# A query phi ahead of the products with 1/den: reordering VectorE and ScalarE in a linear-attention kernel

## The chip, the cores and the metric

One core of a Trainium2 chip (trn2). The metric is the device time of one execution in microseconds; lower is better. Every run quoted here is fast, with a granted TensorE clock of 0.999 or 1.0 (0.996 in one run of before).

Names used throughout: `0q23.phi` is layer 0, query projection, group 2, block 3, the step that ends the feature map phi; `.exp`, `.id1` and `.ts` are the steps ahead of it. `0d02`, `0d23` and the like are the short matmuls (128x8 on a timeline) of such a block (group 0 block 2, group 2 block 3) with `Zm`, the masked sum of the key features; together they make the denominators. `0d0` is the denominator of query group 0, and its three steps are `den` (add and take the reciprocal), `rep` (ScalarE replicates 1/den) and `rT` (a DMA transposes the replica). `0d0.pqn` to `0d0.pqn3` are VectorE's four products of the queries with 1/den. `0G0` to `0G3` are the evacuations of the accumulated matrix G out of PSUM, `0v` the matmuls that use it, `0m` and `0M` the next matmuls and their evacuations, `0r2` the replication of 1/den by matmul, `0w3` the first output tile, and `1u011` the first matmul of the feed-forward layer that follows (`1u011.tanh`, `1x6.sq` and `1x6.vpe` are steps of that layer and of its layer norm). The same code has line numbers that differ by a few between the kernels (L409 and L407, for example).

## The reference

```python
def _A_ref(x, wqkv, wo):          # linear attention, 32 heads of 16
    phi = lambda t: jnp.where(t > 0, t + 1, jnp.exp(t)) + 1e-6
    pq, pk = phi(q), phi(k)
    kv  = jnp.einsum("bhsd,bhse->bhde", pk, v)
    z   = jnp.einsum("bhsd->bhd", pk)
    num = jnp.einsum("bhqd,bhde->bhqe", pq, kv)
    den = jnp.einsum("bhqd,bhd->bhq", pq, z)[..., None] + 1e-6
    return (num / den) @ wo       # heads joined again
# x: 2048 x 512, bf16
x = x + A(layernorm(x));  x = x + B(layernorm(x))   # B: silu(x Wg) * (x Wu) @ Wd, 1792 wide
x = x + A(layernorm(x));  x = x + B(layernorm(x))   # layers 0, 1, 2, 3
```

## The kernel before

The kernel is a list of operations with their reads and writes. TensorE runs them in the order of one list (`PROGRAM`), the other engines each in an order of their own (`ORDER`); waits on semaphores follow from the reads and writes. An engine stops at an operation whose inputs are missing, with all that is behind it: in the profile of before TensorE stood 1.33 us at 0d23; VectorE stood 1.83 us at 0d0.pqn2, and 0q23.phi, whose inputs were ready at about 49.3, started behind it at 51.40; ScalarE stood 1.70 us at 0d1.rep1, to 51.11, and the evacuations of G started behind it at 51.64. The parts that matter here, shortened and simplified:

```python
# phi: exp and, if chosen, "+1" on ScalarE; min and max on VectorE
op("act", exp,  r=[pb], w=[e]);  if on_act: op("act", id1, r=[pb], w=dk)
op("dve", ts,   r=[e],  w=[e])
if on_act: op("dve", phi, r=[e] + dk, w=dk)        # two SBUF inputs
else:      op("dve", phi, r=[pb, e],  w=dk)        # reads PSUM

# den: after the reciprocal, for each of 4 token tiles
q = r_rrep.take()                                   # 3 buffers for 4 tiles: the 4th waits
op("act", rep, r=[rtok], w=[rrep[q]])
op("sp",  rT,  r=[rrep[q]], w=[RT_tl], dma=True)    # DMA transpose
op("dve", pqn, r=ks + [RT_tl], w=ks)                # queries times 1/den
```

```
PROGRAM (TensorE): ... 0q23 0d20 0g15 0g12 0g14 0d23 0d22 0d21 0q30 0v 0q31 0m0..0m3 0r2 0w3 0w2 ...
act:  ... 0d0.rep3 0q23.exp 0q23.id1 0d1.rep1 0G0.evac 0G2.evac 0G3.evac 0d1.rep 0q30.id1 ...
dve:  ... 0q23.ts 0d0.pqn2 0q23.phi 0G1.evac 0d0.pqn1 0d2.den 0d2.den1 0d0.pqn3 0v.mask ...
sp:   ... 0d0.rT 0d0.rT2 0d0.rT1 0d0.rT3 ...
```

Of the kernel before, what the change touches and what calls it, by code (L numbers as in the profile page):

```python
# [8 lines left out]
P = 128  # L9
# [155 lines left out]

PROGRAM = """
# [22 lines left out]
0x14.stats 0x14.sq 0k6.exp 0k7.exp 0k6.id1 0q03.exp 0x11.apply 0k8.id1 0k8.exp 0k15.exp 0k15.id1 0k13.exp 0k12.exp  # L189
0k13.id1 i.c 0k11.exp 0q11.id1 i.c1 0q11.exp 0k14.id1 0k14.exp 0q02.exp 0q02.id1 0q10.exp 0q01.id1 0q01.exp 0q00.exp  # L190
i.c3 0q12.id1 0q12.exp i.c2 0q21.exp 0q21.id1 0q13.id1 0q13.exp 0d0.rep 0d0.rep2 0q20.exp 0d0.rep1 0q22.exp 0d0.rep3
0q23.exp 0q23.id1 0d1.rep1 0G0.evac 0G2.evac 0G3.evac 0d1.rep 0q30.id1 0q30.exp 0q31.exp 0q31.id1 0M1.evac 0M3.evac
0d1.rep3 0d1.rep2 1x3.sq 1x2.sq 0q33.id1 1x1.sq 0q33.exp 1x0.sq 0q32.exp 1x5.sq 0q32.id1 1x11.sq 1x7.sq 1u011.tanh
1u007.tanh 1x6.sq 1u005.tanh 1u008.tanh 1u002.tanh 1u006.tanh 1x6.apply 1x9.sq 1u012.tanh 1u003.tanh 1u013.tanh
# [22 lines left out]
i.c 0x0.stats 0x0.aggr 0x0.vpe 0x1.stats 0x1.aggr 0x0.apply 0x3.stats 0t0.xT 0x4.stats 0x3.aggr 0x4.aggr 0x1.apply  # L217
# [3 lines left out]
0x12.apply 0x14.vpe 0k7.ts 0k6.ts 0k7.phi 0q03.ts 0k9.ts 0k9.phi 0k6.phi 0q03.phi 0x14.apply 0k8.ts 0k12.ts 0k15.ts  # L221
0k8.phi 0k15.phi 0k12.phi 0k13.ts 0k11.ts 0k13.phi 0k11.phi 0k14.ts 0q11.ts 0q02.ts 0k14.phi 0q11.phi 0q02.phi
0q10.ts 0q10.phi 0q01.ts 0q01.phi 0q00.ts 0q00.phi 0z.zm 0q12.ts 0d0.den 0d0.den1 0q13.ts 0q12.phi 0q13.phi 0q21.ts
0q21.phi 0q20.ts 0q20.phi 0d1.den 0q22.ts 0d1.den1 0q22.phi 0q23.ts 0d0.pqn2 0q23.phi 0G1.evac 0d0.pqn1 0d2.den
0d2.den1 0d0.pqn3 0v.mask 0q30.ts 0d2.den2 0d1.pqn1 0M0.evac 0M2.evac 0d0.pqn 0r2.pqn 0w3.res 0r2.pqn1 0w2.res
0r2.pqn2 1x3.apply 0r2.pqn3 0w1.res 1x2.apply 0w0.res 0d1.pqn3 0d1.pqn2 0q33.ts 1x1.apply 0q33.phi 0d1.pqn 0w5.res
1x0.apply 0w11.res 0w9.res 1x5.vpe 0w7.res 0w6.res 0q32.ts 1x5.apply 0w4.res 1x11.vpe 0w10.res 1x7.vpe 1u011.gst
0w8.res 1u011.h 0q31.ts 1x11.apply 0q31.phi 0q30.phi 1u007.gst 1u007.h 1x6.vpe 1u005.gst 1u008.gst 1u008.h 1u005.h
0q32.phi 1u006.gst 1u006.h 1u002.gst 1u002.h 1u012.gst 1x7.apply 1u012.h 1u003.gst 1x4.vpe 0d3.den 1x4.apply 1u003.h
1x9.apply 1u013.gst 0d3.den1 1u013.h 1u010.gst 1u010.h 1u004.gst 1u004.h 1u000.gst 1u000.h 1u001.gst 1u001.h  # L230
1u009.gst 1u009.h 1u110.gst 0d3.pqn 0d3.pqn2 0w14.res 1u110.h 1n3.res 0d3.pqn3 1n1.res 1u102.gst 1n0.res 0w12.res
1u102.h 1n2.res 1u106.gst 1u106.h 0d3.pqn1 2x2.vpe 2x2.apply 1u107.gst 0w13.res 1u204.gst 2x1.vpe 1u107.h 1u101.gst
0w15.res 2x0.vpe 1u204.h 1u101.h 1u111.gst 2x0.apply 1u111.h 1u105.gst 1u109.gst 2k2.ts 1u109.h 2x3.apply 1x14.apply
1u103.gst 1u103.h 1u105.h 1u108.gst 1u108.h 1u104.gst 1u104.h 1u100.gst 1u100.h 1u113.gst 1u112.gst 2k0.ts 1x12.vpe
1u113.h 1u112.h 1n6.res 2k2.phi 1n7.res 2q00.ts 1x15.vpe 1x13.vpe 2k3.ts 2k0.phi 2k0.zs 1u209.gst 2x6.vpe 1x15.apply
1u209.h 1n4.res 1u211.gst 1x12.apply 1u211.h 2x4.vpe 1u205.gst 1n5.res 2x4.apply 1u213.gst 1u205.h 2k1.ts 1u200.gst
1u200.h 1u303.gst 1u213.h 1u202.gst 1u303.h 1u202.h 1u203.gst 1u203.h 1u208.gst 2k1.phi 1u301.gst 1u309.gst 1u208.h
1u301.h 1u304.gst 1u206.gst 1u309.h 1u304.h 1u206.h 1u212.gst 1u212.h 1u201.gst 1u201.h 2k3.phi 1u311.gst 1u311.h
1u302.gst 2q00.phi 2q10.ts 1u302.h 2q11.ts 2q11.phi 1u305.gst 1u305.h 1u207.gst 1u207.h 2q10.phi 1u310.gst 1u310.h
1u308.gst 1u308.h 1u312.gst 1u312.h 1u210.gst 1u210.h 2q02.ts 1n11.res 1u313.gst 1u313.h 2q02.phi 2q01.ts 1u300.gst  # L240
2q03.ts 1n8.res 1u300.h 1n10.res 2x8.vpe 2q03.phi 2k4.ts 2k4.phi 2x10.vpe 1u306.gst 1n9.res 1u306.h 2x11.apply
1u307.gst 2q01.phi 1u307.h 1n14.res 2k8.ts 2k10.ts 2k8.phi 2k8.zs 2k7.ts 2k7.phi 2k10.phi 2k10.zs 1n15.res 2k5.ts
2k6.ts 2k5.phi 2k9.ts 2q21.ts 2x15.vpe 2q21.phi 2k6.phi 2k11.ts 2k11.phi 2x15.apply 2k9.phi 1n13.res 2x13.vpe
1n12.res 2k9.zs 2x13.apply 2q12.ts 2q12.phi 2k15.ts 2k15.phi 2x12.apply 2k14.ts 2k14.phi 2q20.ts 2q20.phi 2k13.ts
2q22.ts 2k13.phi 2q22.phi 2k12.ts 2k12.phi 2k12.zs 2s.zh 2s.zl 2z.zm 2q13.ts 2q23.ts 2q23.phi 2q13.phi 2d0.den
2d0.den1 2d1.den 2q31.ts 2d2.den 2d2.den1 2d0.pqn 2q30.ts 2d1.den1 2d0.pqn1 2q30.phi 2d1.den2 2q31.phi 2G1.evac
2r1.pqn 2d0.pqn2 2r1.pqn1 2v.mask 2r1.pqn2 2r1.pqn3 2M3.evac 2q32.ts 2d0.pqn3 2q33.ts 2w0.res 2q32.phi 2q33.phi
2w2.res 3x0.apply 2w1.res 2d2.pqn3 2d2.pqn 3x2.apply 2w3.res 2w6.res 3x1.apply 2w11.res 2d2.pqn1 3x3.apply 2d2.pqn2
2w5.res 2d3.den 2w8.res 2w7.res 2w4.res 3x11.vpe 3x6.vpe 3x11.apply 2w10.res 3u008.gst 2w9.res 3x6.apply 3u000.gst
3u008.h 3x7.vpe 3u009.gst 3u000.h 3u009.h 3u013.gst 3x5.apply 3u013.h 3x4.apply 3x7.apply 3u010.gst 3u004.gst  # L250
3u010.h 3u004.h 3u003.gst 3u005.gst 2d3.den1 3u005.h 3u003.h 3u007.gst 3u103.gst 3u110.gst 3u007.h 2d3.pqn1 3u103.h
3x9.vpe 3u110.h 2d3.pqn 3u108.gst 3u002.gst 3u108.h 3u012.gst 3u012.h 3u002.h 3u006.gst 3u001.gst 3u006.h 3x9.apply
# [13 lines left out]
0x8.pow 0x15.pow 0x12.pow 0x13.vpe 0x13.pow i.c1 0x13.negm 0x11.pow 0x11.nmr 0x12.negm 0x14.pow 0x14.negm i.ld i.ld1  # L266
i.ld2 i.ld3 i.ld4 i.ld5 i.ld6 i.ld7 i.ld8 i.c7 1x3.negm 1x3.vpe 1x3.pow 1x2.negm 1x2.vpe 1x2.pow 1x1.negm 1x1.vpe
1x1.pow 1x0.negm 1x0.vpe 1x0.pow 1x11.negm 1x5.pow 1x7.negm 1x5.negm Wd.ld3 1x9.negm 1x7.pow 1x6.negm 1x11.pow
Wd.ld1 Wd.ld2 1x4.negm 1x6.pow 1x10.negm Wd.ld 1x6.nmr 1x8.negm 1x9.vpe 1x9.pow 1x4.pow 1x10.vpe 1x10.pow 1x10.nmr
1x8.vpe 1x8.pow 1x8.nmr 2x2.negm 2x0.negm 1x14.negm 2x1.negm 2x2.pow 2x1.pow 2x3.vpe 2x3.negm 2x3.pow 2x0.pow  # L270
2x1.nmr 1x14.vpe 1x14.pow 1x12.pow 2x6.negm 2k2.zs 1x13.negm 1x12.negm 2x7.vpe 1x13.pow 1x15.pow 2x7.negm 1x15.negm
2x7.pow 1x13.nmr 2x6.pow 2x4.pow 2x6.nmr 2x4.negm 2x7.nmr 2x5.vpe 2x5.negm 2x5.pow 2x5.nmr 2k1.zs 2x11.negm 2k3.zs
2x8.negm 2x8.pow 2x8.nmr 2x11.vpe 2x10.negm 2k4.zs 2x11.pow 2x10.pow 2x9.negm 2x10.nmr 2x9.vpe 2x9.pow 2x9.nmr
2x14.negm 2x14.vpe 2x14.pow 2x14.nmr 2k7.zs 2k5.zs 2x15.pow 2x15.negm 2k6.zs 2x13.pow 2x13.negm 2x12.vpe 2x12.pow
2x12.negm 2k11.zs 2k15.zs 2k14.zs 2k13.zs 3x0.negm 3x0.vpe 3x0.pow 3x2.negm 3x2.vpe 3x2.pow 3x1.negm 3x1.vpe 3x1.pow
3x3.negm 3x3.vpe 3x3.pow 3x11.negm 3x11.pow 3x4.negm 3x5.vpe 3x6.negm 3x5.negm 3x6.pow 3x5.pow 3x7.pow 3x7.negm
3x4.vpe 3x4.pow 3x8.vpe 3x8.negm 3x8.pow 3x9.negm 3x9.pow 3x13.negm 3x10.vpe 3x14.negm 3x10.pow 3x12.pow 3x12.negm
3x10.negm 3x10.nmr 3x13.pow 3x13.nmr 3x15.pow 3x14.vpe 3x15.negm 3x14.pow
# [3 lines left out]
0x8.xT 0x15.xT 0x13.xT 0x12.xT 0x11.xT 0x14.xT 0d0.rT 0d0.rT2 0d0.rT1 0d0.rT3 0d1.rT1 0d1.rT 0d1.rT3 0d1.rT2 1x3.xT  # L282
# [8 lines left out]


PE_T = set("""
0d2 0t0 0t1 0t2 0t3 2d1 2z
""".split())



ON_ACT = set("""
0G0 0G2 0G3 0M1 0M3 0k10 0k13 0k14 0k15 0k6 0k8 0k9 0p0 0p11 0p12 0p14 0p7 0q01 0q02 0q11 0q12 0q13 0q21 0q23 0q30  # L300
0q31 0q32 0q33 0s10 0s12 0s13 0s14 0s15 0s2 0s7 0t1 0t12 0t13 0t14 0t2 0t3 0t4 0t5 0t6 0t7 0x11 1p11 1p12 1p13 1p15
1p4 1p5 1p6 1p7 1t0 1t10 1t13 1t14 1t3 1t8 1x10 1x13 1x6 1x8 2G0 2G2 2G3 2M0 2M1 2M2 2b0 2b10 2b12 2b8 2b9 2k0 2k1
2k15 2k2 2k3 2k4 2k5 2k7 2k8 2k9 2p0 2p1 2p10 2p13 2p15 2p2 2p4 2p6 2p8 2q00 2q01 2q02 2q03 2q10 2q11 2q13 2q21 2q22
2q23 2q31 2q32 2q33 2t10 2t14 2t15 2t5 2x1 2x10 2x14 2x5 2x6 2x7 2x8 2x9 3p11 3p12 3p13 3p15 3p6 3p7 3p9 3t0 3t10
3t3 3t4 3t6 3t7 3t8 3x10 3x13
""".split())


def bass_interleave_layers__linear_attn_block__swiglu_ffn__prompt_kernel(
    nc: bass.Bass,  # L310
    A_x: bass.AP,
    A_wqkv: bass.AP,
    A_wo: bass.AP,
    B_x: bass.AP,
    B_w_gate: bass.AP,
# [14 lines left out]
    with stack:  # L330
# [8 lines left out]
        ones = sb("ones", [P, 1], BF16)  # L339
# [240 lines left out]
        def k_proj(L, t):  # L580
# [8 lines left out]
            if f"{L}z" in PE_T:  # L589
                assert L == 0 or all(f"{L - 2}w{i}" in given for i in range(T))  # L590
                z_add(L, t)
# [333 lines left out]
```

## Time and profile before

| | before |
|---|---|
| time, median of the first 3 runs | 429.98 us (429.4 to 430.33) |
| span of the profiled execution | 428.1 us |
| TensorE busy | 419.4 us, 98% |
| longest TensorE idle in the stretch concerned | 1.33 us, ahead of 0d23 |
| stretch from the start of 0d02 to the start of 0w3 | 42.56 to 56.60: 14.04 us |

Busy shares tell only that TensorE sets the time and that there is little idle time to win. What matters is where its idle time lies and who ended it. A timeline line gives start, length, engine, source line, operation, output and inputs, shape and count; in square brackets stands the idle time ahead of it and the operation that ended it. The lines are shown in the prediction.

### The profile page before, as it was taken

Reading aid. Unit: us, or ns where it says so; the run is one execution under the profiler, and the core shown is the slowest. Engines: PE = TensorE matmul, PEld = TensorE weight load, DVE = VectorE, ACT = ScalarE, POOL = GpSimd, SP = SyncE. Lnnn points to the kernel's source line nnn. Section 1 sums busy time; section 2 is a strip of 40 time slices with the busy share of each in tenths; the row PEclk is TensorE's granted clock in tenths of the full one; section 3 lists DMA queues with packets and bytes.
Section 4 is the critical chain, followed back from the end, with each engine's and each line's share of the span. In section 5 each row is a group of like instructions: output and inputs, shape, how many; then the busy total and the mean of one; then the engine's idle time right before and its main releaser. Section 6 shows DMA issues by size and latency. Waiting matters only on the chain.

```text
span 428.1 us, 6340 instructions
## 1 busy us (share of the span) xinstructions
PE 419.4 (98%) x2219; PEld 195.5 (46%) x2219; DVE 287.8 (67%) x629; ACT 202.9 (47%) x399; POOL 83.0 (19%) x205
## 2 busy tenths in 40 slices
PE   8999899999999999999999999999999999999997
PEld 6444444444444444444444444344444444444443
DVE  6865799793675476875447869888837606853662
ACT  5998785563356264254465648445312302402220
POOL 5634035210120150001334500431002000100000
PEclk9999999999999999999999999999999999999999
DMA  8639534522011021000021113322110010021001
GB/s 277 141 75 329 126 64 101 146 50 51 4 22 37 2 52 34 2 0 2 2 48 26 25 26 63 62 46 41 38 38 0 13 51 25 0 63 37 2 0 50
DMA packets 53279, 23.21 MB, mean 54 GB/s; under 512 B 46528, under 2 KB 52160, under 8 KB 53248
## 3 DMA queue, kind: packets, MB, share of 16 engines
q1 hardware_dynamic: 51408, 16.27, 17.6%
q0 software_dynamic: 1296, 6.03, 4.1%
q10 hardware_dynamic: 544, 0.52, 0.4%
q8 instruction: 17, 0.28, 0.3%
q14 instruction: 14, 0.11, 0.1%
HBM read 9.70 MB, written 2.10 MB: 28 GB/s over the span
## 4 chain that ended last, share of the span: by engine, by line
PE 88%; DMA 5%; ACT 3%; DVE 2%; issue 1%; SPq 0%; POOL 0%; ACTq 0%; DVEq 0%
PE pb L409 88%; DMA RT<-rrep 2%; DMA xnT<-xnA 1%; DMA X<-in_A_x_dram 1%; ACT pq L567 1%; ACT etmp L564 1%; ACT rrep L719 0%; DVE pq L573 0%; ACT GT L657 0%; DVE pq L732 0%; SPq L723 0%; ACT xnA L498 0%; SPq L440 0%; DVE xnA L522 0%; ACT xnA L495 0%
## 5 line engine op out<-in xcount | busy, mean ns | idle before, releaser
L782 ACT ACTIVATE tht<-pb 128x512 f32<-128x512 f32 x112 | 65.4, 595 | 129.4 <-PE pb L409 106.8
L409 PE MATMUL pb<-xnT,Wg 128*128 128x512 bf16 x448 | 115.0, 379 | 0.6 <-issue 0.6
L409 PE MATMUL pb<-xnT,Wu 128*128 128x512 bf16 x448 | 115.0, 379 | 0.0
L784 DVE SCALAR_TENSOR_TENSOR tht<-tht,pb 128x512 f32<-128x512 f32 x112 | 75.4, 684 | 55.6 <-ACT tht L782 48.9
L409 PE MATMUL pb<-Wd,hT 128*128 128x512 bf16 (+2 forms) x462 | 99.8, 373 | 0.0
L787 DVE TENSOR_TENSOR hT<-tht,pb 128x512 bf16<-128x512 f32 x112 | 74.2, 682 | 2.8
L409 PEld LDWEIGHTS pb<-Wd,hT 128*128 128x128 bf16 x462 | 44.7, 98 | 52.3 <-DVE hT L787 0.2
L409 PEld LDWEIGHTS pb<-xnT,Wu 128*128 128x128 bf16 x448 | 43.6, 98 | 53.1 <-DVE hT L787 0.8
L409 PEld LDWEIGHTS pb<-xnT,Wg 128*128 128x128 bf16 x448 | 43.5, 98 | 53.3 <-issue 1.3
L511 POOL TENSOR_TENSOR rstd<-vpe,negh 128x1 f32<-128x1 f32 x64 | 37.4, 587 | 90.4 <-DVE vpe L507 88.3
L564 ACT ACTIVATE etmp<-pb 128x512 bf16<-128x512 f32 x64 | 37.2, 594 | 21.8 <-PE pb L409 13.1
L501 POOL TENSOR_SCALAR mv<-sums 128x1 f32<-128x1 f32 x55 | 12.8, 239 | 119.8 <-DVE X L810 62.1
L409 PE MATMUL pb<-Wqkv,xnT 128*128 128x512 bf16 x128 | 31.2, 379 | 1.2 <-DMA xnT<-xnA 0.6
L409 PE MATMUL pb<-xnT,Wqkv 128*128 128x512 bf16 x128 | 32.1, 379 | 0.0
L409 PE MATMUL pb<-pk,xnA 128*128 128x512 bf16 x128 | 31.2, 379 | 0.0
L409 PE MATMUL pb<-GT,pq 128*128 128x512 bf16 x128 | 30.2, 379 | 0.2
L498 ACT ACTIVATE xnB<-X,sums 128x512 bf16<-128x512 bf16 x32 | 22.9, 717 | 15.7 <-DVE X L762 8.8
L569 DVE TENSOR_SCALAR etmp<-etmp 128x512 bf16<-128x512 bf16 x64 | 18.7, 304 | 12.1 <-ACT etmp L564 12.0
L762 DVE SCALAR_TENSOR_TENSOR X<-pb,X 128x512 bf16<-128x512 f32 x32 | 21.6, 686 | 7.1 <-PE pb L409 7.0
L810 DVE SCALAR_TENSOR_TENSOR X<-pb,X 128x512 bf16<-128x512 f32 x16 | 11.0, 689 | 19.1 <-PE pb L409 19.0
L498 ACT ACTIVATE xnA<-X,sums 128x512 bf16<-128x512 bf16 x23 | 16.5, 717 | 12.1 <-DVE X L810 11.9
L810 DVE SCALAR_TENSOR_TENSOR pq<-pb,X 128x512 bf16<-128x512 f32 (+2 forms) x17 | 10.9, 656 | 14.4 <-PE pb L409 14.3
(77 smaller groups left out, 309.9 us busy)
## 6 DMA issues: line engine op xcount, KB each, us to landing
out_dram<-pq SPq DMA_DIRECT2D x15, 128.0 KB, 1.8
Wg<-in_B_w_gate_dram POOLq DMA_DIRECT2D x4, 448.0 KB, 4.9
Wu<-in_B_w_up_dram POOLq DMA_DIRECT2D x4, 448.0 KB, 4.6
X<-in_A_x_dram SPq DMA_DIRECT2D x6, 256.0 KB, 4.8
Wd<-in_B_w_down_dram POOLq DMA_DIRECT2D x3, 512.0 KB, 4.7
Wqkv<-in_A_wqkv_dram SPq DMA_DIRECT2D x2, 512.0 KB, 7.0
Wqkv<-in_A_wqkv_dram ACTq DMA_DIRECT2D x2, 256.0 KB, 3.5
X<-in_A_x_dram SPq DMA_DIRECT2D x4, 128.0 KB, 3.4
```

Of the source, the lines that this page charges most:

```text
L409: return op("pe", lambda e: e.matmul(o_ap, lhsT=lhsT, rhs=rhs, start=start, stop=stop, skip_group_check=skip), r=r, w=w, n=n)
L498: op("act", lambda a: a.activation(out=b_ap, in_=X[:, t, :], func=ACT.Square, scale=-float(D), bias=sums[:, t:t + 1], accum_out=mv[:, t, 1 ...
L501: op("pool", lambda p: p.tensor_scalar(out=mv[:, t, 0:1], in0=sums[:, t:t + 1], scalar1=-1.0 / D, scalar2=None, op0=ALU.mult), r=[f"sm{t}" ...
L511: op("pool", lambda p: p.tensor_tensor(out=rstd[:, t:t + 1], in0=vpe[:, t:t + 1], in1=negh[:], op=ALU.pow), r=[f"vp{t}", "negh"], w=[f"rs{ ...
L564: op("act", lambda a: a.activation(out=etmp[e][:], in_=PB[pb][:], func=ACT.Exp), r=[f"pb{pb}"], w=[f"e{e}"], kind="exp")
L567: op("act", lambda a: a.activation(out=dst, in_=PB[pb][:], func=ACT.Identity, bias=onep[:]), r=[f"pb{pb}", "onep"], w=dk, kind="id1")
L569: op("dve", lambda v: v.tensor_scalar(out=etmp[e][:], in0=etmp[e][:], scalar1=1.0, scalar2=1e-6, op0=ALU.min, op1=ALU.add), r=[f"e{e}"], w ...
L762: op("dve", lambda v: v.scalar_tensor_tensor(out=X[:, t, :], in0=PB[pb][:], scalar=1.0, in1=X[:, t, :], op0=ALU.mult, op1=ALU.add, accum_o ...
L782: op("act", lambda e: e.activation(out=tht[a][:], in_=PB[pg][:], func=ACT.Tanh, scale=0.5), r=[f"pb{pg}"], w=[f"th{a}"], kind="tanh")
L784: op("dve", lambda v: v.scalar_tensor_tensor(out=tht[a][:], in0=tht[a][:], scalar=1.0, in1=PB[pg][:], op0=ALU.add, op1=ALU.mult), r=[f"pb{ ...
L787: op("dve", lambda v: v.tensor_tensor(out=hT[h][:, j, :], in0=tht[a][:], in1=PB[pu][:], op=ALU.mult), r=[f"pb{pu}", f"th{a}"], w=[f"h{h}_{ ...
L810: op("dve", lambda v, pb=pb, lo=lo, hi=hi: v.scalar_tensor_tensor(out=o_ap[:, lo:hi], in0=PB[pb][:, 0:hi - lo], scalar=0.5, in1=X[:, t, lo ...
```

## The change

It is meant to let the last query phi that TensorE needs (0q23.phi) run before VectorE takes up the products with the first 1/den, and to evacuate G before ScalarE turns to the second 1/den. Neighbouring operations on all engines are rearranged with it, up to about 75 us. TensorE's list stays word for word, and the `z_mm` part of the diff only rewrites how the sums for z are emitted. The core of the diff (cut; `...` stands for what is left out):

```diff
 act
-0d0.rep3 0q23.exp 0q23.id1 0d1.rep1 0G0.evac 0G2.evac 0G3.evac 0d1.rep 0q30.id1 ...
+0q23.exp 0d0.rep3 0G0.evac 0G1.evac 0G3.evac 0d1.rep 0d1.rep1 0q30.id1 ...
-1u011.tanh 1u007.tanh 1x6.sq 1u005.tanh
+1u007.tanh 1u011.tanh 1x6.sq 1u005.tanh
 dve
-0q23.ts 0d0.pqn2 0q23.phi 0G1.evac 0d0.pqn1 0d2.den 0d2.den1 0d0.pqn3 0v.mask
+0q23.ts 0q23.phi 0d0.pqn 0G2.evac 0d2.den 0d0.pqn1 0d2.den1 0v.mask 0d0.pqn3
 sp
-0d0.rT 0d0.rT2 0d0.rT1 0d0.rT3 0d1.rT1 0d1.rT
+0d0.rT 0d0.rT1 0d0.rT2 0d0.rT3 0d1.rT 0d1.rT1
 ON_ACT
-0G2 0k15 0q23 ...   +0G1 0k11 ...      (0q23.phi now reads PSUM)
 ... (many more moves of the same kind ahead of and behind these)
```

## The prediction

> **What bounds the kernel now.** I read the page first (busy times, slices), then the chain of waits that ended last, then the timeline from 42 to 72 us engine by engine, then the DMA window from 48 to 51.1 us.
>
> ```profile
> PE 419.4 (98%) x2219; PEld 195.5 (46%) x2219; DVE 287.8 (67%) x629; ACT 202.9 (47%) x399; POOL 83.0 (19%) x205
> PE   8999899999999999999999999999999999999997
> PEclk9999999999999999999999999999999999999999
> ```
>
> TensorE is busy 419.4 of 428.1 us at full clock. Only the 8.7 us in which it idles can be won by reordering: 8.7 / 430 = 2.0%, all of it, start and end included. The chain of waits tells where:
>
> ```profile
> 45.23 1.19 SPq L723
> ...
> 46.51 4.53 DMA RT<-rrep
> 51.04 0.02 issue
> 51.06 0.04 DVE pq L732
> ...
> 51.40 0.43 DVE pq L573
> 51.83 0.05 issue
> 51.88 3.15 PE pb L409 x36
> ```
>
> One DMA transpose of the replicated 1/den (line 723) takes 4.53 us, then VectorE multiplies by it (L732), then makes a query phi (L573), and only then TensorE goes on. The timeline of PE and of VectorE there:
>
> ```profile
> 47.79 2.75 PE L409 MATMUL pb<-pk,xnA 128*128 128x512 bf16 x12
> 51.88 0.46 PE L409 MATMUL pb<-Zm,pq 128*128 128x8 bf16 x12 [1.33 <-DVE pq L573]
> ```
> ```profile
> 48.94 0.28 DVE L569 TENSOR_SCALAR etmp<-etmp 128x512 bf16<-128x512 bf16 x1
> 51.06 0.43 DVE L732 TENSOR_TENSOR pq<-pq,RT 128x512 bf16<-128x512 bf16 x1 [1.83 <-DMA RT<-rrep]
> 51.40 0.42 DVE L573 TENSOR_TENSOR pq<-pq,etmp 128x512 bf16<-128x512 bf16 x1
> ```
>
> VectorE's list says 0q23.ts, 0d0.pqn2, 0q23.phi. The product 0d0.pqn2 waits for its transpose, and 0q23.phi, whose inputs were ready at about 49.3 (ScalarE's id1 ran 48.73 to 49.3), stands behind it. TensorE needs that phi for 0d23. ScalarE loses the same stretch to the same transpose: 0d1.rep1 reuses a buffer that it reads, and the evacuations of G stand behind it:
>
> ```profile
> 51.11 0.63 ACT L719 ACTIVATE rrep<-rtok 128x512 bf16<-128x512 bf16 x1 [1.70 <-issue]
> 51.64 1.55 ACT L657 ACTIVATE GT<-pb 128x512 bf16<-128x512 f32 x3
> ```
>
> Why 4.53 us, where transposes elsewhere take 2.4? In the DMA window 48 to 51.1, beside the transposes' small packets, there is one large one:
>
> ```profile
> q8 instruction: 1, 0.02, 1.9%
> ```
>
> In the trace's landings, 15 of the 16 increments of this transpose came by 48.94 and the last at 51.04; the one 16 KB instruction packet ran 49.03 to 49.98. I read it as a collision on one DMA engine. The queue has 17 such packets (0.28 MB), [...] so it should return at the same place of TensorE's program, changed or not.
>
> [...] I count PE gaps between starts (512-column matmuls start 0.216 us apart: 12 in 2.59) and not from busy ends. By this the gap ahead of 0d23 is 51.88 - (47.79 + 2.59) = 1.50, not 1.33.
>
> **The change, part by part.** TensorE's program list is the same word for word. What the heading calls work ahead of the fourth key tile (0g0, 0g1 before 0k3) is already there, and the z_mm part of the diff yields the same matmuls. All that changes is the order on ScalarE, VectorE, GpSimd and SP up to about 75 us, plus a few operations moved from one engine to another.
>
> 1. VectorE: 0q23.phi ahead of all products with the first 1/den; the first of these is now 0d0.pqn, whose transpose landed at 47.63. 0q23 also loses ScalarE's id1, so its phi is the 0.63 us form from PSUM instead of 0.43. Walk from VectorE's Zm at 42.30, with spacings from the timeline (ts 0.21, phi from PSUM 0.6, tensor-tensor 0.34, reciprocal 0.87): den 43.18, reciprocal done 44.63 (0.17 later, because 0q21.ts is inserted), 0q12.phi done 46.15 (TensorE wants it at 46.53: slack 0.38), 0q20.phi 47.0, 0q22.phi 48.2, second reciprocal 49.1, 0q23.phi 49.95. TensorE reaches 0d23 at 47.79 + 2.59 = 50.38. **The 1.50 us gap goes.**
> 2. ScalarE: evacuations of G now precede 0d1.rep and rep1. The last accumulation starts at 49.5 and its four banks fill by 50.58; G0, G1, G3 on ScalarE from 49.95 at 0.5 each end at 51.46, G2 on VectorE at 51.0. TensorE does 0d2x (0.31) and 0q30 (0.86) until 51.55, so 0v starts there (53.05 before).
> 3. 0v 0.94 and 0q31 0.86 end at 53.35. v.mask: 52.69 to 53.3. VectorE in between: 0d2.den, 0d0.pqn1, reciprocal, done by 52.5, provided that pqn1's transpose lands by 51.25. It is issued at about 46.75, and even with the same late increment (51.04) it fits. 0m starts at 53.45 (55.03 before), ends 54.31.
> 4. ScalarE in the meantime: rep, rep1, then 0q30 and 0q31 with two passes each, (51.46 + 6 x 0.53) = 54.6. The fourth matmul of 0r2 reuses the bank that 0q31.exp reads last, so 0r2 loses about 0.3 and ends at 55.25 (56.60 before). M1 and M3 end at 55.6, the last needed at 55.7: 0w3 is held for some 0.2 and ends at 56.11. Before, it started at 56.60 and four matmuls end at 57.46. **Net: 57.46 - 56.11 = 1.35 us.** Before, 50.38 to 56.60 held 6.22 us for 4.45 us of spacing, 1.77 lost; after, 0.4 of it stays.
> 5. Is it kept? TensorE has no visible gap from 56.6 to 98. Tightest places when moved 1.35 forward: 0w11 at 60.43 needs 0r2.pqn3, walked to 60.12; 1u011 at 67.45 needs the last transpose of 1x0, whose apply moved ahead of w5.res and pqn, ending 64.6 (65.98 before, landing 68.46), so landing 67.1. 1u007.tanh now precedes 1u011.tanh on ScalarE, delaying u011.h to 72.6, wanted at 74.36. All hold by 0.3 us or more. After that, the lists are the old ones and everything moves with TensorE.
> 6. The three copies of esel move to about 28 on ScalarE (3 x 0.65); it has caught up by 37.15, where 0q10.exp ran before at 37.14. The tightest bank need, 0q01 for 0k14.id1, holds by 0.5. Off the path. So are x1.apply ahead of x4.aggr and the moved vpe (0.15 each): TensorE's next stop, at 15.69, waits for a transpose that starts with x4.apply at 9.3 either way.
>
> Sum: 429.98 - 1.35 = 428.6.
>
> **The rivals.** (a) The late increment belongs to the profiled execution and not to the timed ones. Then 0d0.pqn2 could start at about 49.2, there was no gap to win, and the time stays at 429.7 or so. For it: a DMA accident, and three runs spread over 0.9 us. Against: [...] the profiled run took 429.86, as the others. One in five. (b) A new wait takes the place of the old: ScalarE's six passes ahead of M1 and M3, or 0d0.pqn1 and pqn3 standing ahead of v.mask and M0.evac when their transposes come late. Slacks are 0.2 to 0.6, so a slip of 1 us would make 429.4. One in five. (c) All slips go well and the 0.4 left over goes too: 428.2. (d) A lost bank or late xnT at 1u011 that makes it slower than before, 430.5: one in twenty.
>
> **Range and chances.** Centre 428.7, a little above the sum because (a) and (b) pull upward; 427.9 to 429.9 also allows for the 0.4 us by which medians of three can move. A 2% change is 8.6 us, all of PE's idle time: 0.01 for faster. Slower by as much would need a stall six times the one removed: 0.01.
>
> **What would show it.** Right: PE's 1.33 us gap ahead of the 128x8 matmuls near 50.4 is gone, 0q23's phi is the form from PSUM and comes before any L732, 0v starts near 51.6, 0w3 near 55.3, 1u011 near 67.5, and the instruction packet is still at 49, now harmless. Wrong: a PE gap between 51.5 and 56 behind ScalarE or L732 of over 0.6 us (rival b), a gap ahead of 1u011 (d), or a kernel before whose other executions lack the late increment (a).

## The result, and the profile after

| | before | changed |
|---|---|---|
| first rounds, median (runs) | 429.69 us (4) | 429.30 us (4) |
| ratio of these rounds | | 0.9991 (0.9974 to 1.0008) |
| repeated later, median (runs) | 429.71 us (10) | 428.68 us (5) |
| ratio of these rounds | | 0.9984 (0.9970 to 0.9998) |
| span of the first profile | 428.1 us | 427.3 us |

The ratios are those for the fast runs of the same rounds; they are not quite the ratios of the medians. The brackets hold a 95% interval. The change is worth between nothing and 1.3 us by the timing, most likely 0.4 to 0.7 us (1 - 0.9991 and 1 - 0.9984 of about 429.7).

Busy time and clock on the page of the changed kernel:

```profile
PE 418.4 (98%) x2219; PEld 194.8 (46%) x2219; DVE 288.3 (67%) x628; ACT 201.8 (47%) x398; POOL 82.6 (19%) x206
...
PEclk9999999999999999999999999999999999999999
```

As before, TensorE is 98% busy at full clock (granted clock 1.0 in both profiles). The timeline of TensorE in the changed kernel, from the last accumulation of G to the first output tile:

```profile
48.53 2.75 PE L407 MATMUL pb<-pk,xnA 128*128 128x512 bf16 x12
51.11 0.45 PE L407 MATMUL pb<-Zm,pq 128*128 128x8 bf16 x12
...
52.28 1.06 PE L407 MATMUL pb<-GT,Wqkv 128*128 128x128 bf16 x16
...
54.12 1.04 PE L407 MATMUL pb<-Wo,KVT 128*128 128x512 bf16 x4
...
55.79 1.90 PE L407 MATMUL pb<-GT,pq 128*128 128x512 bf16 x8
```

The last accumulation starts at 48.53; twelve 512-column matmuls at 0.216 us between starts take 2.59 us, and 0d23 starts right there, at 51.11. The bracket with 1.33 us is gone, and so is any other on these lines. VectorE and ScalarE at the same place:

```profile
50.10 0.69 DVE L574 SCALAR_TENSOR_TENSOR pq<-pb,etmp 128x512 bf16<-128x512 f32 x1
50.71 0.41 DVE L731 TENSOR_TENSOR pq<-pq,RT 128x512 bf16<-128x512 bf16 x1
51.10 0.69 DVE L659 CAST GT<-pb 128x512 bf16<-128x512 f32 x1
```
```profile
50.67 1.58 ACT L656 ACTIVATE GT<-pb 128x512 bf16<-128x512 f32 x3 [0.93 <-PE pb L407]
52.11 1.16 ACT L718 ACTIVATE rrep<-rtok 128x512 bf16<-128x512 bf16 x2
```

0q23.phi is now the form that reads PSUM (`pq<-pb,etmp`, 0.69 us), and it precedes the first product (L731). ScalarE's evacuations of G start as soon as TensorE has the banks ready (0.93 us waited for PE) and no longer behind a replication.

The DMA window from 48.5 to 52 us of the changed kernel still has the large instruction packet in it:

```profile
q8 instruction: 1, 0.02, 1.7%
```

It began at 49.46, after 693 of TensorE's 4438 matmul and weight-load records; in before at 49.03, after 695. Each of the 17 packets began within 38 records of the same packet in the other profile; on average there is one packet per 261 records (4438 / 17).

The stretch from 0d02 to 0w3 fell from 14.04 to 12.50 us (43.29 to 55.79), that is by 1.54. But the whole span fell by only 0.8, because 0d02 started later, at 43.29 in place of 42.56:

```profile
43.29 0.56 PE L407 MATMUL pb<-Zm,pq 128*128 128x8 bf16 x16 [0.36 <-DVE Zm L614]
```

Did the change make the head longer, or do two executions just differ by that much? The experiments had to answer this too.

### The profile page after: what moved, and what is told of

It reads as the page before. It is cut to its first block, busy times and chain, and to the rows that moved or that the text cites. A ratio compares the mean times of both kernels' runs of the same rounds, so it can differ in the third digit from the quotient of the medians.

```text
span 427.3 us, 6331 instructions
## 1 busy us (share of the span) xinstructions
PE 418.4 (98%) x2219; PEld 194.8 (46%) x2219; DVE 288.3 (67%) x628; ACT 201.8 (47%) x398; POOL 82.6 (19%) x206
## 4 chain that ended last, share of the span: by engine, by line
PE 85%; DMA 6%; DVE 3%; ACT 2%; issue 2%; SPq 1%; POOL 1%; POOLq 0%; ACTq 0%; DVEq 0%
PE pb L407 85%; DMA xnT<-xnA 2%; DMA Wu<-in_B_w_up_dram 1%; DMA Wo<-in_A_wo_dram 1%; DMA X<-in_A_x_dram 1%; ACT etmp L562 1%; SPq L722 1%; DMA xnT<-xnB 1%; DMA RT<-rrep 1%; ACT GT L656 0%; ACT rrep L718 0%; DVE stats L486 0%; DVE xnA L520 0%; POOL rstd L509 0%; DVE X L761 0%
## 5 line engine op out<-in xcount | busy, mean ns | idle before, releaser
L499 POOL TENSOR_SCALAR mv<-sums 128x1 f32<-128x1 f32 x55 | 12.5, 234 | 116.7 <-DVE X L809 61.9
```

The costliest lines, as they stand in the source:

```text
L499: op("pool", lambda p: p.tensor_scalar(out=mv[:, t, 0:1], in0=sums[:, t:t + 1], scalar1=-1.0 / D, scalar2=None, op0=ALU.mult), r=[f"sm{t}" ...
```

## The experiments

Twelve runs followed, all correct; c1 and c2 repeat the two kernels unchanged. Each was timed beside the kernel before and profiled once; the last round (e5, e7, e9, e10) ran on another chip than the two rounds ahead of it. In the table, "head" is the start of 0d02, followed by the three stretches in which the rest of the execution can be split; "2nd" and "4th" are the landings of the second and the fourth transpose of 0d0 in the queue: the time of the 15th of their 16 semaphore increments and, after the slash, of the 16th. The first two rows are the two profiles already seen. The last stretch is taken from a span given to 0.1 us, so it is good to 0.05 us.

| kernel | head | 0d02 to 0w3 | 0w3 to 1u011 | 1u011 to end | 2nd | 4th | ratio |
|---|---|---|---|---|---|---|---|
| before | 42.56 | 14.04 | 12.20 | 359.30 | 48.94 / 51.04 | 52.31 / 52.33 | |
| changed | 43.29 | 12.50 | 12.28 | 359.23 | 49.91 / 51.46 | 53.42 / 53.44 | 0.9991 |
| c1 before again | 42.74 | 13.55 | 12.20 | 359.21 | 49.09 / 50.73 | 52.64 / 52.65 | 0.9996 |
| e1 phi only | 42.62 | 13.70 | 12.20 | 359.08 | 49.18 / 50.75 | 52.58 / 52.59 | 0.9986 |
| e2 evac only | 42.90 | 13.82 | 12.19 | 359.09 | 49.25 / 51.19 | 53.15 / 53.16 | 0.9995 |
| e3 phi and evac | 43.32 | 13.09 | 12.41 | 359.58 | 49.66 / 51.49 | 53.45 / 53.46 | 0.9987 |
| e9 three moves | 43.46 | 13.22 | 12.42 | 359.20 | 49.90 / 51.84 | 53.74 / 53.75 | 0.9993 |
| c2 changed again | 42.25 | 12.49 | 12.26 | 359.70 | 50.55 / 50.58 | 52.47 / 52.49 | 0.9984 |
| e4 late product first | 42.41 | 14.20 | 12.25 | 359.24 | 49.03 / 50.81 | 52.75 / 52.76 | 1.0008 |
| e5 landed product first | 43.41 | 12.50 | 12.28 | 359.71 | 50.09 / 51.69 | 53.62 / 53.63 | 0.9984 |
| e6 before, packet moved | 42.98 | 13.42 | 12.53 | 360.67 | 49.33 / 49.35 | 51.98 / 53.97 | 1.0037 |
| e7 changed, packet moved | 42.60 | 12.51 | 12.56 | 362.23 | 49.24 / 49.24 | 51.89 / 53.81 | 1.0043 |
| e8 changed, mask early | 42.31 | 12.49 | 12.25 | 359.95 | 48.95 / 50.55 | 52.48 / 52.50 | 0.9982 |
| e10 later waits | 43.02 | 12.49 | 12.25 | 359.04 | 49.66 / 51.46 | 53.38 / 53.40 | 0.9969 |

The 95% intervals of the ratios reach 0.0012 to 0.0017 to either side.

### c1: the kernel before, once more

> The kernel before once more, unchanged: what two executions differ by. My theory (the wait is in every execution): the 16th increment of the second 1/den transpose again comes about 2 us after the 15th, the gap of 1.3 us ahead of 0d23 is there again, 14.0 us lie between the starts of 0d02 and 0w3 (42.56 to 56.60 before), and 371.5 from there to the end. Rival a (accident of one profile): no gap, about 12.5 to 13. The head, up to 0d02, took 42.56 in the one profile of before and 43.29 in the one of after; if that is noise of the first loads, this run's head may lie anywhere from 42.3 to 43.5; if the change caused it, at 42.5. Ratio 1.000.

No edit. Median 429.41 us, before beside it 429.70 (9 runs): the same kernel read 0.9996, within its interval of 1. TensorE's line at 0d23:

```profile
51.56 0.46 PE L409 MATMUL pb<-Zm,pq 128*128 128x8 bf16 x12 [0.84 <-DVE pq L573]
```

The wait was there again, and the last increment late again (50.73), but the wait was 0.84 us, not 1.33, and the stretch 13.55, not 14.04. So the wait is no accident of one profile; its size moves by half a microsecond from execution to execution. The head was 42.74, and across the six kernels with the old head (before, c1, e1, e2, e3, e9) it ran from 42.56 to 43.46, mean 42.93.

### e1 and e2: either move alone

```diff
 e1, dve
-0q23.ts 0d0.pqn2 0q23.phi
+0q23.ts 0q23.phi 0d0.pqn2
 e2, act
-0q23.id1 0d1.rep1 0G0.evac 0G2.evac 0G3.evac
+0q23.id1 0G0.evac 0G2.evac 0G3.evac 0d1.rep1
```

> Before, with 0q23.phi alone moved ahead of 0d0.pqn2 on VectorE. My theory: TensorE's gap ahead of 0d23 goes (1.5 us by starts), but ScalarE still evacuates G only behind 0d1.rep1, which waits for the same transpose, so 0v can't finish before about 53.9 and 0r2 waits for ScalarE as before: 0d02 to 0w3 shrinks by only 0.1 to 0.3 us (13.8). Rival: VectorE's order was the whole of it, and this alone gives 1.3 to 1.5 us (12.5).

> Before, with the three evacuations of G alone moved ahead of 0d1.rep1 on ScalarE. My theory: the gap ahead of 0d23 stays at 1.3 us and 0d02 to 0w3 stays within 0.2 of 14.0. Rival: ScalarE's order was the whole of it, and this gives 1.3 us or more (12.6).

In e1 the wait ahead of 0d23 went, and TensorE waited for the evacuations of G instead. TensorE's timeline, then ScalarE's:

```profile
52.48 0.23 PE L409 MATMUL pb<-GT,Wqkv 128*128 128x128 bf16 x1 [0.20 <-ACT GT L657]
52.96 0.90 PE L409 MATMUL pb<-GT,Wqkv 128*128 128x128 bf16 x13 [0.26 <-ACT GT L657]
```
```profile
50.82 0.63 ACT L719 ACTIVATE rrep<-rtok 128x512 bf16<-128x512 bf16 x1 [1.18 <-issue]
51.35 1.55 ACT L657 ACTIVATE GT<-pb 128x512 bf16<-128x512 f32 x3
```

The two brackets are the G banks that come late (L657); ScalarE's own line shows why: the replication ahead of them stood 1.18 us (by its times it ends with the second transpose's last increment at 50.75, which frees the replica's buffer). The stretch was 13.70, between the two profiles of before. In e2 the wait ahead of 0d23 stayed:

```profile
52.03 0.46 PE L409 MATMUL pb<-Zm,pq 128*128 128x8 bf16 x12 [1.14 <-DVE pq L573]
```

with a stretch of 13.82. Each half alone is hidden by the other. Timed, e1 read 0.9986 (429.15 us) and e2 0.9995 (429.50 us); e1's ratio is lower than its profile would have it, by an amount the timing can't separate from noise.

### e3: both moves, and e9: a third

> Both moves of the two runs ahead, nothing else of the change. My theory: together they give what neither gives alone: 0d02 to 0w3 falls to 12.4 to 12.8 us, as in the changed kernel (12.50), and the time falls by 1.2 to 1.5 us, ratio 0.9965 to 0.9972, if the head is as in before. Rival: the other moves of the change carry the gain, and this gives less than half of it.

The two edits above together gave 13.09 us: more than either alone, less than the 12.4 to 12.8 expected. TensorE's timeline has a new wait ahead of 0m0:

```profile
55.09 1.02 PE L409 MATMUL pb<-Wo,KVT 128*128 128x512 bf16 x4 [0.61 <-DVE KVT L669]
```

The mask product (L669) stood on VectorE behind 0d0.pqn3, whose transpose landed at 53.46. So e9 added one more move:

```diff
 e9 = e3 and, dve
-0d0.pqn3 0v.mask
+0v.mask 0d0.pqn3
```

> Before with three moves: 0q23.phi ahead of 0d0.pqn2, the evacuations of G ahead of 0d1.rep1, and now also the mask product ahead of 0d0.pqn3, for which TensorE waited 0.61 us in the run of the first two. My theory: these three are the change's whole gain; 0d02 to 0w3 is 12.4 to 12.8 us as in the changed kernel (12.50, 12.49), against 13.09 with two. Rival: the order of the transposes on SP or the other moves matter as well: 12.9 or more.

The stretch did not come down: 13.22 us. My account of three moves was incomplete. VectorE's timeline in e9:

```profile
51.87 0.43 DVE L732 TENSOR_TENSOR pq<-pq,RT 128x512 bf16<-128x512 bf16 x1 [1.05 <-DMA RT<-rrep]
52.21 0.69 DVE L660 CAST GT<-pb 128x512 bf16<-128x512 f32 x1
```

0d0.pqn2, the product of the late transpose, is still the first of the four, and one evacuation of G (L660) stands behind it. It starts at 52.21 and holds 0v on TensorE:

```profile
52.95 1.01 PE L409 MATMUL pb<-GT,Wqkv 128*128 128x128 bf16 x15 [0.28 <-DVE GT L660]
```

The reciprocal and the mask product behind it are late in turn. That e9 is no shorter than e3 lies in the late increment, which came 8.38 us after 0d02 in e9 and 8.17 in e3; from that increment to 0w3 it was 4.84 and 4.92 us. The changed kernel begins with 0d0.pqn instead, the product of the first transpose, and puts the evacuation right after it. By these lines, that order of the products, with the matching order of the transposes on SP, is the part of the gain (13.1 to 12.5) that the moves of the phi and of the evacuations don't bring. No run made that change alone, and the changed kernel differs in other moves too, so this part is argued and not shown. Timed, e3 read 0.9987 (429.04 us) and e9 0.9993 (429.17 us).

### e4 and e5: a product back ahead of the phi

```diff
 e4, changed kernel, dve
-0q23.ts 0q23.phi 0d0.pqn 0G2.evac 0d2.den 0d0.pqn1
+0q23.ts 0d0.pqn1 0q23.phi 0d0.pqn 0G2.evac 0d2.den
 e5, changed kernel, dve
-0q23.ts 0q23.phi 0d0.pqn 0G2.evac
+0q23.ts 0d0.pqn 0q23.phi 0G2.evac
```

> The changed kernel with one product put back ahead of 0q23.phi: 0d0.pqn1, whose transpose is second in the queue and had the late last increment (51.46) in the changed kernel's profile. My theory: VectorE waits for it to about 51.3, 0q23.phi ends near 52.4, and TensorE has a gap of 1.2 to 1.5 us ahead of 0d23: 0d02 to 0w3 is 13.7 to 14.1 us. Rival: any place of the products does, as ScalarE's order is what counts: below 13.0.

> The changed kernel with 0d0.pqn put back ahead of 0q23.phi: a product too, but of the first transpose, whose 16 increments came together in every profile (47.35 to 48.41), long before VectorE gets there (about 50). My theory (what cost time was the one late transpose, not that a product stood ahead of the phi): 0d23 is delayed by 0.1 us at most and 0d02 to 0w3 stays at 12.4 to 12.8, against 14.20 with 0d0.pqn1 there. Rival (any product ahead of the phi costs): 13 or more.

e4's VectorE, then its TensorE:

```profile
50.84 0.42 DVE L731 TENSOR_TENSOR pq<-pq,RT 128x512 bf16<-128x512 bf16 x1 [1.66 <-DMA RT<-rrep]
51.18 0.68 DVE L574 SCALAR_TENSOR_TENSOR pq<-pb,etmp 128x512 bf16<-128x512 f32 x1
```
```profile
51.92 0.46 PE L407 MATMUL pb<-Zm,pq 128*128 128x8 bf16 x12 [1.53 <-DVE pq L574]
```

The product of the late transpose waited 1.66 us, the phi followed it, TensorE stood 1.53 us, and the stretch was 14.20: the whole gain was gone. The timing shows it too: e4's four executions took 429.88 to 430.08 us, the five of c2 in the same round 428.35 to 429.72. In e5 a product stood ahead of the phi as well, but one whose transpose had landed at 48.54. No wait ahead of 0d23 appeared (TensorE's line has no bracket) and the stretch was 12.50, as in the changed kernel.

```profile
51.24 0.45 PE L407 MATMUL pb<-Zm,pq 128*128 128x8 bf16 x12
```

What costs is one late transpose with the phi behind it, not a product ahead of the phi.

### e6 and e7: where the lateness comes from

```diff
 TensorE's list, first 42 warm-up matmuls
-S x42        (128x128 on 128 columns)
+D x21        (128x128 on 256 columns: 21 matmuls and 21 weight loads fewer; 0t0 starts at 5.67 us, in before at 5.72)
```

> Before, with the 42 warm-up matmuls at the start replaced by 21 of twice the width: the same TensorE time there, but 42 instructions fewer (a matmul and a weight load each)[...], and nothing else moves. My theory (the late increment comes from the instruction packet): the packet near 49 moves to about 53 to 54, all 16 increments of the second transpose come within 0.2 us of each other, near 49, the gap ahead of 0d23 goes, and 0d02 to 0w3 is 12.5 to 13.0 us with no change of any order on VectorE or ScalarE. Rival: the lateness has another cause (the SP queue, the last weight loads): the 16th increment stays 1.5 to 2 us late and 0d02 to 0w3 stays at 13.5 to 14.0.

> The changed kernel with the 21 wide warm-up matmuls of the run with the old order. There the instruction packet moved from 49 to 51.5, the late increment from the second transpose to the fourth (51.98, then 53.97), and TensorE waited 1.18 us for the mask product, which stood behind the fourth transpose's product. My theory: the packet moves the same way, but in the changed order the mask product precedes that product, so TensorE has at most a short wait ahead of 0r2 or 0w3, and 0d02 to 0w3 is 12.4 to 13.0 us. Rival: the late fourth transpose costs here too, as M0's evacuation stands behind its product: 13.3 or more. The whole time may be longer, as it was with the old order (431.07), from packets that fall elsewhere later.

In e6, the kernel before with nothing reordered, the instruction packets moved from 13.48, 32.77 and 49.03 to 21.61, 37.22 and 51.48, with 42 of TensorE's instructions fewer ahead of them. The second transpose then had all its increments between 49.21 and 49.35, and TensorE ran through 0d23 without a wait. This is the test of the collision: the lateness followed the packet. All 14 profiles agree in a further number: the transpose that met the packet (the second, in e6 and e7 the fourth) had its last increment 1.04 to 1.18 us after the packet's end, whether the packet took 0.94 or 1.40 us (all 17 packets took 0.94 to 1.37 us in before and 0.92 to 1.26 in changed). Where no packet met them, the first and the last increment of these transposes were 0.14 to 0.21 us apart in those two profiles. And in the profile of before the small packets of the transposes ran at 3 or 4 per 0.1 us from 49.8 to 50.7, against about 80 before that: from this I infer that one of the page's 16 DMA engines worked off its share behind the packet. That was not shown: which engine a packet used is not in the trace. The lateness did not vanish, though, as I had expected; the packet moved by 2.5 us and not from 49 to 53 or 54 (my estimate), and hit the fourth transpose, whose last increment came at 53.97, 2 us behind the 15th. The DMA window from 51.1 to 54.2 us of e6 has the packet:

```profile
q8 instruction: 1, 0.02, 2.8%
```

VectorE and TensorE of e6:

```profile
53.99 0.42 DVE L732 TENSOR_TENSOR pq<-pq,RT 128x512 bf16<-128x512 bf16 x1 [1.20 <-DMA RT<-rrep]
54.33 0.68 DVE L669 TENSOR_TENSOR KVT<-pb,mask 128x512 bf16<-128x512 f32 x1
```
```profile
50.81 0.45 PE L409 MATMUL pb<-Zm,pq 128*128 128x8 bf16 x12
...
55.07 1.04 PE L409 MATMUL pb<-Wo,KVT 128*128 128x512 bf16 x4 [1.18 <-DVE KVT L669]
```

VectorE waits 1.20 us for the product of the fourth transpose, the mask product (L669) stands behind it, and TensorE waits 1.18 us for that: the same mechanism at another place, and a stretch of 13.42, outside the 12.5 to 13.0 expected. In e7 the changed kernel met the same late fourth transpose (51.89, then 53.81) and its stretch was 12.51. There the mask product precedes that product. So in both places tried, the changed order takes the late increment without a wait. Both kernels were nevertheless slower as a whole (431.07 and 431.74 us): 1.4 and 3 us more from 1u011 to the end. One part of it is a wait of TensorE near 271 us for a product with 1/den of layer 2 (1.26 us in e6, 1.75 in e7). The kept traces fit the same collision there. VectorE in e6:

```profile
271.18 0.76 DVE L732 TENSOR_TENSOR pq<-pq,RT 128x512 bf16<-128x512 bf16 x2 [1.49 <-DMA RT<-rrep]
```

In e6 the packet ran from 268.24 to 269.47, and the transpose for that product, issued at 266.98, landed at 271.15, with all 16 increments late (from 270.79 on); in e7 the packet ran from 267.52 to 269.27 and the transpose, issued at 266.20, landed at 270.87. In before the packet (265.65 to 266.91) met an earlier transpose there, issued at 263.78 and landed at 268.08, for which TensorE did not wait. The changed orders end at about 75 us, so they can't help there.

### c2: the changed kernel, once more

> The changed kernel once more, unchanged. My theory: the stretch from 0d02 to 0w3 is again 12.4 to 12.8 us, against 14.04, 13.55 and 13.82 in the three profiles so far of kernels with the old order there; and the head up to 0d02, which took from 42.56 to 43.32 in five profiles of kernels with the old head, lies anywhere from 42.5 to 43.4. Time 1.0 to 1.3 us below before, ratio 0.997 to 0.998. Rival: the change also lengthens the head (43.29 in its first profile), so that it is again 43.2 or more, and the ratio stays at 0.999.

Median 428.68 us, before 429.71 (10 runs), ratio 0.9984. The stretch was 12.49, as in the first profile, and the head 42.25. The four kernels with the changed head (changed, c2, e4, e5) had heads from 42.25 to 43.41, mean 42.84, against 42.93 for the old: no lengthening of the head is seen. The 0.73 us lost there in the first pair of profiles lie within the spread of either group. In c2, the 16 increments of the second transpose came late together (50.51 to 50.58), with the packet at 48.44; that didn't hurt either. Two of the expectations were missed by little: the head was below 42.5, and the ratio above 0.998.

With these profiles one can see what set the stretch. In before, c1, e1 and e2, 0w3 started 5.53 to 5.57 us after the last increment of the second transpose, which itself came 7.99 to 8.48 us after 0d02: the increment fixed the stretch, and this is why it moved by half a microsecond. In the changed kernel, c2, e5, e8 and e10 (the last two below) that increment came 8.17 to 8.44 us after 0d02 and the stretch stayed 12.49 to 12.50.

### e8 and e10: towards a faster version

```diff
 e8, changed kernel, pool
-i.ld ... i.ld8 i.c7        (nine weight loads, then the last step of the mask)
+i.c7 i.ld ... i.ld8
 e10 = e8 and
 act  -1u007.tanh 1u011.tanh 1x6.sq 1u005.tanh
      +1u011.tanh 1u007.tanh 1u005.tanh 1x6.sq
 dve  -1u011.h 1x6.vpe 1u007.gst 1u005.gst 0q31.phi 1u007.h
      +1u011.h 0q31.phi 1u007.gst 1u005.gst 1u007.h 1x6.vpe
```

> The changed kernel with the last step of the mask ahead of GpSimd's nine weight loads in place of behind them. In the profiles so far the product Zm waited for that step, and TensorE's 0d02 stood 0.2 to 0.5 us for Zm. My theory: 0d02 follows 0q13 at once (0.86 to 0.9 us between the starts, 1.38 in the changed kernel), and all behind it moves forward by 0.3 to 0.5 us: 0.4 us faster than the changed kernel run again beside it. Rival: the next wait (second 1/den transpose, ScalarE's passes ahead of M1) takes it back: no gain at 0w3.

> An attempt at a faster version: the changed kernel with the mask early, and with the wait ahead of 0d31 taken away that this mask run showed (0.66 us: 0q31.phi stood on VectorE behind work that waited for 1x6's square on ScalarE, which waited for a transposed buffer). 1u011.tanh again ahead of 1u007.tanh, 1x6.sq behind 1u005.tanh, 0q31.phi ahead of 1u007.gst, 1x6.vpe behind 1u007.h. My theory: no wait ahead of 0d31 even with a late transpose; 0d02 to 0w3 stays 12.5, 1u011 to the end 359.2 to 359.7, time 0.3 to 0.6 us below the changed kernel. Rival: the noise of the first loads and of later packets is larger than this; the ratio can't be told from the changed kernel's.

In e8 GpSimd makes the mask at 24.75 (42.56 in the changed kernel), and 0d02 follows 0q13 after 0.86 us (1.38 in the changed kernel's first profile, 0.99 in c2). But the time, 428.76 us, was that of c2 (428.68), and not 0.4 us below it. In its profile 0.66 us were lost later, ahead of 0d31. TensorE's line and ScalarE's in e8:

```profile
78.45 0.26 PE L406 MATMUL pb<-Zm,pq 128*128 128x8 bf16 x4 [0.66 <-DVE pq L570]
```
```profile
72.62 0.72 ACT L495 ACTIVATE xnB<-X,sums 128x512 bf16<-128x512 bf16 x1 [1.70 <-DMA xnT<-xnB]
```

1x6.sq on ScalarE waits 1.70 us for a transposed buffer, 1x6.vpe on VectorE waits for it, and 0q31.phi stands behind. e5 and e7 had a wait at the same place (0.62 and 0.52 us); the changed kernel's own two profiles and e4 had none. e10 reorders these as well. Its TensorE at 0d02:

```profile
42.16 1.02 PE L405 MATMUL pb<-xnT,Wqkv 128*128 128x512 bf16 x4
43.02 0.55 PE L405 MATMUL pb<-Zm,pq 128*128 128x8 bf16 x16
```

No wait for Zm, none ahead of 0d31, and 359.04 us from 1u011 to the end. But the transposed buffer landed 4.76 us after 1u011 here, nearly as early as in the changed kernel (4.63), and not 5.28 to 5.49 us as in e5, e7 and e8; so whether the new order would stand a late one was not tested. The median was 428.57 us, ratio 0.9969 (0.9956 to 0.9983) to before: the lowest of all; of the others, only e1, c2 and e8 have an interval wholly below 1. Its interval overlaps those of the changed kernel, which wasn't timed in the same rounds (c2 ran on another chip); that it beats before is shown, that it beats the changed kernel is not.

## Why the prediction was right or wrong

The prediction was 428.7 us, range 427.9 to 429.9; measured were 429.3 and, repeated, 428.68. It was right in the range, and its mechanism was confirmed. The range alone says little: it also holds the 429.69 us of before, so that no change at all would have fallen into it. The gain was overestimated: 1.3 us were forecast (428.7 against 429.98), and the timing gives 0.4 to 0.7. The confirmation lies in the positions below.

- **What bounds the kernel, and the collision.** Right. The late increment came in c1, e1 and e2 again, and e4 is slower than c2 in the timed executions too, so rival (a) falls; and it moved with the instruction packet in e6 (from 49.03 to 51.48). That packet and transpose met on one DMA engine is my reading and was not shown.
- **Steps 1 to 4, the walk.** Right, in positions relative to 0d02. Predicted and measured in the first profile: 0d23 at 7.82 and 7.82 us, 0v at 8.99 and 8.99, 0m at 10.89 and 10.83, 0w3 at 12.69 and 12.50. The reasons hold one by one: e4 undoes step 1 and brings the wait back; e1 and e2 show that steps 1 and 2 need each other; e3, in the old order, shows what a late product ahead of the mask costs (0.61 us), the worry of rival (b). That the order of the products seems to count in its own right (e9) the walk contained, as it used the new list, but the text did not say it.
- **The 1.35 us of step 4.** The sum has a slip: it names a hold of 0.2 us ahead of 0w3, but 56.11 is 55.25 plus four matmuls, without it. By luck this did no harm, as no hold came; and 0m to 0w3 grew by only 0.10 us (1.57 to 1.67) and not by 0.3. The size fits the first pair of profiles (14.04 to 12.50, with 0.08 lost again up to 1u011). But it took the one profile of before for all executions. With c1 the old stretch is 13.80 on average, and the new one 12.50, so the gain is 1.30 there, with a spread of half a microsecond.
- **Step 5, "is it kept?"** Here the working failed in part. From 1u011 to the end, the four profiles with the changed order took 359.47 us on average (changed, c2, e4, e5), the six with the old one (before, c1, e1, e2, e3, e9) 359.24; each group spreads by 0.5 us. The difference of 0.23 is as large as two waits, spread over four profiles: c2's 0.31 us ahead of 0w14 at 96.78, and e5's 0.62 ahead of 0d31. The first is not the change's doing: e3, with the old order there, has it too (0.28 us). The second came in e5, e7 and e8 and in none of the seven profiles with the old order. The prediction named the swap of 1u007.tanh and 1u011.tanh, but looked only at what needs u011.h and not at 1x6.sq and 0q31.phi behind it when a transpose is late. That this swap makes the wait is not shown. So up to 0.2 us of the gain may be given back later, with 0.07 more between 0w3 and 1u011.
- **The sum.** 1.30 - 0.07 - 0.23 = 1.0 us by the profiles (a little more if c2's wait is not counted), against 1.35 predicted and 0.4 and 0.7 timed. Both intervals of the timing hold 1.0. What of the remaining 0.3 to 0.6 is noise and what is a cost that the profiles missed stays open.
- **The head.** The prediction had it unchanged; c2 and the means of 42.93 and 42.84 bear that out. Step 6 (the copies of esel off the path) is in agreement with it; it was not tested alone.

## What to carry to other kernels

On an engine that works its list in order, as VectorE and ScalarE do here (in before they stood 1.83 and 1.70 us, to 51.06 and 51.11, with the last increment of one transpose at 51.04), look at each operation that waits for a DMA and ask what stands behind it that TensorE needs soon; put those first. Taking the transfers' products in the order in which the transfers were issued belonged to the change too, but was not tested alone. When one transfer takes much longer than its like, look at when each of its increments came: here it was one of sixteen, 1.55 to 2.10 us behind the fifteenth (in c2 all sixteen came late together), and its time could be read from the end of an instruction packet, 1.04 to 1.18 us before it. With an engine in order behind that transpose TensorE stood 0.84 to 1.53 us (c1 and e4). A gain of 0.3% can't be read from a few timings that spread by as much; the length of the changed stretch, in several profiles, shows it clearly.
